# The last store of an attention decode kernel: one transfer of four rows against four transfers of one row from two engines

## The chip, the cores and the metric

The kernel runs on one core of a Trainium2 chip. The metric is the device time of one execution in microseconds (us). Times of whole executions come from repeated runs; everything finer comes from one profiled execution of each kernel. Two spans are used: the whole time, and **the tail**, which is the time from the end of VectorE's copy of the result to the end of the profiled span. The tail is all that the change can touch. An **issue** is the instruction by which an engine starts a transfer. A transfer's data leave in **packets**; in these stores each has a small packet beside it that writes a semaphore. A store is called **confirmed** here when that write has **landed**.

## The reference

One token passes through a layer normalisation; then the results of two branches are added to it: attention with 32 query heads over 8 cached key/value heads of 65,536 keys each, and a small feed-forward network.

```python
def reference(A_x, A_k_cache, A_v_cache, A_wq, A_wo, B_x, B_w1, B_b1, B_w2, B_b2):
    x = A_x                                  # (1, 1, 512) bf16
    xn = _layernorm(x, axis=-1)
    # _A_ref: q = xn @ wq; scores over 65536 cached keys; softmax; times V; @ wo
    # _B_ref: gelu(xn @ w1 + b1) @ w2 + b2
    return x + _A_ref(xn, A_k_cache, A_v_cache, A_wq, A_wo) + _B_ref(xn, B_w1, B_b1, B_w2, B_b2)
```

The caches hold 256 MiB; the output is 512 numbers of 2 bytes, 1 KB.

## The kernel before

The kernel streams keys and values through on-chip memory, and at the end multiplies the attention output with `wo`. The products go to four rows of one accumulator, at partitions 0, 32, 64 and 96, each row a quarter of the output. VectorE copies them to a tile `fin_bf`, and SyncE stores the four rows in one transfer:

```python
    for kt in range(KT):                                   # KT == 4
        ... pR[32 * kt:32 * kt + 1, 0:128] accumulates output columns kt*128 .. kt*128+127
    NR = 32 * (KT - 1) + 1
    sch.op(DVE, lambda: dve.tensor_copy(out=fin_bf[0:NR, :], in_=pR[0:NR, 0:128]),
           reads=[f"pss{R}"], writes=["fin"])
    ev_out = sch.dma(
        SP,
        lambda: sp.dma_start(out=out[0, 0].rearrange("(kt p) -> kt p", p=128), in_=fin_bf[0:NR:32, :]),
        sem_out, reads=["fin"], writes=["out_dram"],
    )
    # ... cut: the engines' programs are emitted in one block; what follows the
    # last placement of the attention output is emitted after it
    for e, obj in ((PE, pe), (DVE, dve), (SP, sp)):
        _emit(obj, e.ops[rest[e]:])
    sp.wait_ge(ev_out.sem, ev_out.val)
```

`sch.dma` and `sch.op` record an instruction with the semaphore waits that its reads and writes need. The kernel ends when SyncE's wait for the store's semaphore is over.

Of the kernel before, what the change touches and what calls it, by code (L numbers as in the profile page):

```python
# [154 lines left out]
def _fold(bodies, each):  # L155


    n = len(bodies)
    assert n >= 3 and all(len(b) == len(bodies[0]) for b in bodies)
    seen = {}  # L160
    for i, b in enumerate(bodies):
        for k, (waits, _, _) in enumerate(b):
            for s, v in waits:
                seen.setdefault((k, s), {})[i] = v
    growth = dict(each)
    for (_, s), at in seen.items():
        if n - 1 in at and n - 2 in at:
            assert growth.setdefault(s, at[n - 1] - at[n - 2]) == at[n - 1] - at[n - 2]
    out = []
    known = {}  # L170
    for k in range(len(bodies[0])):
        assert len({(b[k][2] or (None, 0))[1] for b in bodies}) == 1
        need = {}
        for (kk, s), at in seen.items():
            if kk == k:
                need[s] = max(v - i * growth.get(s, 0) for i, v in at.items())
        waits = [(s, v) for s, v in need.items() if known.get(s) is None or known[s] < v]
        for s, v in waits:
            known[s] = v
            assert v >= 1  # L180
        out.append((waits, bodies[0][k][1], bodies[0][k][2]))
    return out, growth


def _emit(eng_obj, ops):
    for waits, fn, pub in ops:
        for s, v in waits:
            eng_obj.wait_ge(s, v)
        if fn is None:
            continue  # L190
        ins = fn()
        if pub is not None:
            ins.then_inc(pub[0], pub[1])


def _emit_rolled(eng_obj, ops, marks, each, holder=None, step=None):
    folded, growth = _fold([ops[a:b] for a, b in zip(marks, marks[1:])], each)
    _emit(eng_obj, ops[:marks[0]])
    _emit_loop(eng_obj, folded, growth, len(marks) - 1, holder, step)
    _emit(eng_obj, ops[marks[-1]:])  # L200


def _emit_loop(eng_obj, ops, growth, n, holder, step):

    uses = {}
    for waits, _, _ in ops:
        for s, v in waits:
            uses.setdefault(s, []).append(v)
    regs, steps = {}, []
    at = {}  # L210
    for s, vs in uses.items():
        grow = growth.get(s, 0)
        key = (vs[0], grow) if len(vs) == 1 else s
        if key not in regs:
            r = eng_obj.alloc_register(f"w{len(regs)}")
            eng_obj.reg_mov(r, vs[0])
            regs[key] = r
            steps.append((r, vs[0] + grow - vs[-1]))
        at[s] = [regs[key], vs[0]]
    with eng_obj.Fori(0, n) as index:  # L220
        if holder is not None:
            holder[0] = index
        for waits, fn, pub in ops:
            for s, v in waits:
                r, now = at[s]
                if v != now:
                    eng_obj.reg_add(r, r, v - now)
                    at[s][1] = v
                eng_obj.wait_ge(s, r)
            ins = fn()  # L230
            if pub is not None:
                ins.then_inc(pub[0], pub[1])
        for r, by in steps:
            eng_obj.reg_add(r, r, by)
        if step is not None:
            step()
    if holder is not None:
        holder[0] = None


def bass_parallel_sum__gqa_block_cached__dense_activation_gelu__decode_kernel(
# [21 lines left out]
    KT = D // 128  # L263
# [23 lines left out]
    sch = _Sched(nc)  # L287
    PE = sch.add_engine("pe", "pe", is_pe=True)
    DVE = sch.add_engine("dve", "dve")
    ACT = sch.add_engine("act", "act")  # L290
    POOL = sch.add_engine("pool", "pool")
    SP = sch.add_engine("sp", "sp")
# [4 lines left out]
    pe = nc.tensor  # L297
    dve = nc.vector
    act = nc.scalar
    pool = nc.gpsimd  # L300
    sp = nc.sync

    def sb(name, shape, dt):
        return nc.alloc_sbuf_tensor(name, shape, dt)
# [34 lines left out]
    fin_bf = sb("fin_bf", [128, 128], BF)  # L339
# [57 lines left out]
    sem_w1 = sch.dsem("dw1")  # L397
    sem_w2 = sch.dsem("dw2")
    wsem = [sch.dsem(f"wsem{i}") for i in range(sum(len(s) for s in WS))]
    sem_out = sch.dsem("dout")  # L400

    for t, res in ((ident_bf, "ident_bf"), (ident_f, "ident_f")):
        sch.op(POOL, lambda t=t: pool.memset(t[:, :], 0.0), writes=[res])
# [3 lines left out]
                out=t[:, :], in_=t[:, :], compare_op=ALU.not_equal, fill=1.0,  # L407
                base=0, pattern=[[-1, 128]], channel_multiplier=1,
            ),
            reads=[res], writes=[res],  # L410
# [178 lines left out]
    def k_setup():  # L589
        trace = nc.cur_bb.bb.instructions  # L590
        n = len(trace)
        zero = pe.alloc_register("kzero")
        pe.reg_mov(zero, 0)
        tile = kv[:, bass.ds(pe.snap(zero, min_val=0, max_val=PCOL), DH)]
        kreg["ap"] = pe.transpose(pst[0][:, 0:128], tile, ident_bf[:, :]).ins.ins[1]
        assert trace[-2].outs[0].regref == kreg["ap"].regref
        kreg["at"] = trace[-2].ins[1].value
        del trace[n:]
        kreg["base"] = pe.alloc_register("kbase")
        kreg["both"] = pe.alloc_register("kboth")  # L600
        kreg["tile"] = [pe.alloc_register(f"ktile{r}") for r in range(NREG)]
        pe.reg_mov(kreg["base"], kreg["at"])
        pe.reg_mov(kreg["both"], 2 * kreg["at"] + 2 * PCOL)
# [159 lines left out]
    def place(w):  # L763
        ws = slice(w * WR, (w + 1) * WR)
        sch.op(PE, lambda: pe.matmul(pO[:, PO_X + w * WR:PO_X + (w + 1) * WR], lhsT=oM_bf[:, w, :],
                                     rhs=part_r[:, :], start=True, stop=True),
               reads=[f"oM{w}", "part_r"], writes=["pO0"])
        sch.op(DVX, lambda: dve.tensor_copy(out=oX_bf[:, ws], in_=pO[:, PO_X + w * WR:PO_X + (w + 1) * WR]),
               reads=["pO0"], writes=[f"oX{w}"])
# [52 lines left out]
    for t, res, pat in ((part_m, "part_m", "p (a r) -> p a r"), (part_r, "part_r", "p (a r) -> p r a")):  # L822
        sch.op(DVE, lambda t=t, pat=pat: dve.tensor_reduce(
            out=t[:, :], in_=ident_f[:, :].rearrange(pat, r=WR), axis=AX.X, op=ALU.max),
            reads=["ident_f"], writes=[res])
    marks, marks2 = [], []
    for i in range(NU // 2):
# [5 lines left out]
        each = {e.sem: e.count - was[e.sem] for e in (PE, DVE, ACT)}  # L833
# [10 lines left out]
    def fin_mm(kt, lhsT, rhs, reads, first, last, publish):  # L844
        sch.op(PE, lambda: pe.matmul(pR[32 * kt:32 * kt + 1, 0:128], lhsT=lhsT, rhs=rhs, start=first, stop=last),
               reads=reads, writes=[f"pss{R}"], publish=publish)
# [3 lines left out]
    for w in range(NW):  # L850
        if w:
            place(w)
            rest = {e: len(e.ops) for e in (PE, DVE, SP)}
        for r0, r1 in WS[w]:
            end = w == NW - 1 and r1 == WR
            for r in range(r0, r1):
                for kt in range(KT):
                    fin_mm(kt, oX_bf[:, w * WR + r:w * WR + r + 1], wo_sb[:, w * WR + r, kt * 128:(kt + 1) * 128],
                           [f"oX{w}", f"wo{w}_{r0}"], False, end and r == WR - 1, r == r1 - 1 and kt == KT - 1)
    NR = 32 * (KT - 1) + 1  # L860
    sch.op(DVE, lambda: dve.tensor_copy(out=fin_bf[0:NR, :], in_=pR[0:NR, 0:128]),
           reads=[f"pss{R}"], writes=["fin"])
    ev_out = sch.dma(
        SP,
        lambda: sp.dma_start(out=out[0, 0].rearrange("(kt p) -> kt p", p=128), in_=fin_bf[0:NR:32, :]),
        sem_out, reads=["fin"], writes=["out_dram"],
    )

    first, SP.ops[0] = SP.ops[0], ([], None, None)
    assert not first[0]  # L870
# [9 lines left out]
    with nc.Block() as block:  # L880

        @block.gpsimd
        def _(e):
            _emit(e, POOL.ops)

        @block.sync
        def _(e):
            _emit(e, SP.ops[:rest[SP]])

        @block.scalar  # L890
        def _(e):
            _emit_rolled(e, ACT.ops, [m[1] for m in marks2], each)

        @block.vector
        def _(e):
            _emit_rolled(e, DVE.ops[:rest[DVE]], [m[0] for m in marks2], each, pair)

        @block.tensor
        def _(e):
            k_setup()  # L900
            _emit_rolled(e, PE.ops[:rest[PE]], marks, each, step=k_step)

    for e, obj in ((PE, pe), (DVE, dve), (SP, sp)):
        _emit(obj, e.ops[rest[e]:])
    sp.wait_ge(ev_out.sem, ev_out.val)


# [26 lines left out]
```

## Time and profile before

| | before |
|---|---|
| time, median of 3 runs | 655.79 us (655.75 to 655.83) |
| profiled span | 654.3 us |
| read from memory | 280.50 MB at 429 GB/s |
| end of the result copy to the end of the span (tail) | 1.705 us |

The difference of some 1.5 us between time and span lies outside the profile's span. The page's DMA row and the chain, both shown in the prediction, say that the loads set the pace until about 651.6 us; after that there are eight matmuls, one copy and the store.

### The profile page before, as it was taken

Reading aid. Unit: us, or ns where it says so; the run is one execution under the profiler, and the core shown is the slowest. Engines: PE = TensorE matmul, PEld = TensorE weight load, DVE = VectorE, ACT = ScalarE, POOL = GpSimd, SP = SyncE. Lnnn points to the kernel's source line nnn. Section 1 sums busy time; section 2 is a strip of 40 time slices with the busy share of each in tenths; the row PEclk is TensorE's granted clock in tenths of the full one; section 3 lists DMA queues with packets and bytes.
Section 4 is the critical chain, followed back from the end, with each engine's and each line's share of the span. In section 5 each row is a group of like instructions: output and inputs, shape, how many; then the busy total and the mean of one; then the engine's idle time right before and its main releaser. Section 6 shows DMA issues by size and latency. Waiting matters only on the chain.

```text
span 654.3 us, 29016 instructions
## 1 busy us (share of the span) xinstructions
PE 530.7 (81%) x12681; PEld 504.3 (77%) x12681; DVE 280.6 (43%) x571; ACT 249.7 (38%) x454; POOL 5.6 (1%) x74
## 2 busy tenths in 40 slices
PE   2488498696969959697895969879596996998997
PEld 0187498696969959696895969779595986998996
DVE  3145063361625436162542616345261633645363
ACT  0134053351625425152451615335161543535351
POOL 0000000000000000000000000000000000000000
PEclk9688597695958869597885959779595887969695
DMA  9999999999999999999999999999999999999997
GB/s 386 445 430 439 415 452 431 421 441 441 429 441 421 441 429 441 425 437 449 421 425 441 441 425 433 433 441 433 437 425 437 433 441 421 425 445 421 427 439 310
DMA packets 6791, 280.66 MB, mean 429 GB/s; under 512 B 890, under 2 KB 1020, under 8 KB 1276
## 3 DMA queue, kind: packets, MB, share of 16 engines
q1 hardware_dynamic: 6632, 280.50, 99.4%
q8 instruction: 8, 0.13, 0.1%
q10 hardware_dynamic: 148, 0.01, 0.0%
q14 instruction: 3, 0.02, 0.0%
HBM read 280.50 MB, written 0.00 MB: 429 GB/s over the span
## 4 chain that ended last, share of the span: by engine, by line
DMA 57%; PE 33%; DVE 3%; another core or an unknown queue 3%; ACT 2%; issue 2%; SPq 1%; POOL 0%; ACTq 0%; DVEq 0%
DMA kv<-in_A_k_cache_dram 41%; PE pst L581 16%; DMA kv<-in_A_v_cache_dram 9%; DMA kv<-in_A_wo_dram 6%; PE pss L629 5%; PE pA L698 4%; PE pO L698 4%; DVE pmax L637 1%; DMA rows_bf<-in_A_x_dram 1%; PE pA L656 1%; ACT kt_ring L620 1%; PE pA L667 1%; DVE kt_ring L618 1%; PE pO L517 1%
## 5 line engine op out<-in xcount | busy, mean ns | idle before, releaser
L581 PE MATMUL pst<-ident_bf,kv 128*128 128x128 bf16 x4096 | 335.0, 233 | 87.2 <-POOL flag L449 84.6
L581 PEld LDWEIGHTS pst<-ident_bf,kv 128*128 x4096 | 261.7, 104 | 89.1 <-issue 89.0
L620 ACT ACTIVATE kt_ring<-pst 128x1024 bf16<-128x1024 bf16 x192 | 196.4, 1023 | 315.2 <-PE pst L581 300.3
L618 DVE COPY kt_ring<-pst 128x1024 bf16<-128x1024 bf16 x320 | 217.2, 690 | 222.5 <-PE pst L581 222.4
L629 PE MATMUL pss<-q_cur,kt_ring 128*128 128x4 bf16 x4096 | 174.5, 165 | 3.2 <-issue 1.7
L629 PEld LDWEIGHTS pss<-q_cur,kt_ring 128*128 128x128 bf16 x4096 | 153.9, 97 | 9.5 <-issue 5.5
L680 ACT ACTIVATE P_bf<-pss,negm 128x128 bf16<-128x128 f32 x128 | 57.1, 546 | 57.0 <-DVE negm L670 57.0
L698 PE MATMUL pO<-P_bf,kv 128*128 128x4 bf16 x2048 | 60.4, 166 | 5.8 <-issue 4.0
L698 PEld LDWEIGHTS pO<-P_bf,kv 128*128 128x128 bf16 x2048 | 56.5, 100 | 10.4 <-issue 8.3
L698 PEld LDWEIGHTS pA<-P_bf,kv 128*128 128x128 bf16 x2048 | 60.2, 106 | 4.7 <-issue 3.6
L698 PE MATMUL pA<-P_bf,kv 128*128 128x4 bf16 x2048 | 59.4, 167 | 4.5 <-issue 3.6
L680 ACT ACTIVATION_READ_ACCUMULATOR P_bf<-pss,negm 128x1 f32 x128 | 35.1, 274 | 0.0
L713 DVE COPY o_all<-pO 128x4 f32 (+1 forms) x16 | 2.6, 161 | 54.2 <-PE pO L720 54.2
L637 DVE TENSOR_REDUCE pmax<-pss 128x4 f32<-128x512 f32 x32 | 21.9, 685 | 7.2 <-PE pss L629 7.2
L713 DVE COPY o_all<-pA 128x4 f32 (+1 forms) x16 | 2.6, 161 | 38.2 <-PE pA L698 38.2
L656 PE MATMUL pA<-ident_f,pmax 128*4 128x128 f32 x64 | 13.0, 288 | 3.9 <-DVE pmax L637 2.6
L667 PE MATMUL pA<-diag,ones_f 4*128 4x4 f32 x64 | 13.6, 281 | 0.0
L658 DVE TENSOR_REDUCE gmax<-pA 4x1 f32<-4x128 f32 x32 | 8.8, 274 | 10.6 <-PE pA L656 10.6
L667 PEld LDWEIGHTS pA<-diag,ones_f 4*128 4x128 f32 x64 | 10.8, 210 | 2.0
L670 DVE TENSOR_SCALAR negm<-pA 128x4 f32<-128x4 f32 x32 | 5.2, 161 | 13.5 <-PE pA L667 13.5
L510 PE MATMUL pA<-ones_bf,xn_row 1*128 1x1 bf16 x4 | 0.3, 172 | 12.7 <-DVE xn_row L506 12.7
L510 PEld LDWEIGHTS pA<-ones_bf,xn_row 1*128 1x128 bf16 x4 | 0.2, 114 | 12.7 <-DVE xn_row L506 12.7
(78 smaller groups left out, 80.8 us busy)
## 6 DMA issues: line engine op xcount, KB each, us to landing
kv<-in_A_k_cache_dram SPq DMA_DIRECT2D x6, 4096.0 KB, 37.4
kv<-in_A_v_cache_dram SPq DMA_DIRECT2D x6, 4096.0 KB, 22.1
kv<-in_A_wq_dram SPq DMA_DIRECT2D x1, 4096.0 KB, 12.2
kv<-in_B_w_dram SPq DMA_DIRECT2D x2, 1792.0 KB, 17.7
kv<-in_A_wo_dram SPq DMA_DIRECT2D x1, 2048.0 KB, 34.5
kv<-in_A_wo_dram SPq DMA_DIRECT2D x1, 1152.0 KB, 36.8
kv<-in_A_wo_dram SPq DMA_DIRECT2D x1, 512.0 KB, 37.6
kv<-in_A_wo_dram SPq DMA_DIRECT2D x1, 256.0 KB, 37.8
```

What stands on the lines that cost most here:

```text
L517: sch.op(PE, lambda: pe.matmul(out, lhsT=lhsT, rhs=rhs, start=first, stop=last), reads=reads, writes=[res], publish=publish)
L581: ins = pe.transpose(pst[tb][:, at * 128:(at + 1) * 128], kslot[0][:, t, :], ident_bf[:, :]).ins
L618: e, fn = DVE, lambda tb=tb, dst=dst: dve.tensor_copy(out=dst, in_=pst[tb][:, :])
L620: e, fn = ACT, lambda tb=tb, dst=dst: act.activation(out=dst, in_=pst[tb][:, :], func=ACTF.Copy)
L629: lambda k=k, kb=kb, at=at, t=t: pe.matmul(pss[k][:, at:at + HPG], lhsT=kt_ring[:, kb * FCOL + t * 128:kb * FCOL + (t + 1) * 128], rhs=q_c ...
L637: lambda k=k: dve.tensor_reduce(out=pmax[:, :], in_=pss[k][:, 0:CW].rearrange("p (t j) -> p j t", j=HPG), axis=AX.X, op=ALU.max),
L656: sch.op(PE, lambda: pe.matmul(pA[0:HPG, PA_ST:PA_ST + 128], lhsT=pmax[:, 0:HPG], rhs=ident_f[:, :], start=True, stop=True), reads=["pmax" ...
L658: sch.op(DVE, lambda: dve.tensor_reduce(out=gmax4[:, :], in_=pA[0:HPG, PA_ST:PA_ST + 128], axis=AX.X, op=ALU.max), reads=["pA"], writes=[" ...
L667: sch.op(PE, lambda: pe.matmul(pA[:, PA_SB:PA_SB + HPG], lhsT=ones_f[0:HPG, 0:128], rhs=diag4[0:HPG, 0:HPG], start=True, stop=True), reads ...
L670: sch.op(DVE, lambda us=us: dve.tensor_scalar(out=negm[:, us], in0=pA[:, PA_SB:PA_SB + HPG], scalar1=-1.0, scalar2=None, op0=ALU.mult), re ...
L680: lambda: act.activation(out=P_v[k][:, :, j], in_=src[:, :, j], func=ACTF.Exp, bias=negm[:, at:at + 1], scale=1.0, accum_out=sums[:, at:at ...
L698: lambda k=k, t=t: pe.matmul(acc[:, 0:HPG], lhsT=vslot[:, k * TPD + t, :], rhs=P_v[k][:, t, :], start=t == 0, stop=t == TPD - 1),
```

## The change

The intent is to shorten the one issue of 0.64 us on SyncE: four transfers of a single row each, alternately issued by ScalarE and SyncE, so that each engine issues two. Each engine's transfers share a semaphore, and SyncE waits for both at the end.

```diff
-    sem_out = sch.dsem("dout")
+    sem_out = [sch.dsem(f"dout{i}") for i in range(2)]
...
-            rest = {e: len(e.ops) for e in (PE, DVE, SP)}
+            rest = {e: len(e.ops) for e in (PE, DVE, SP, ACT)}
...
-    ev_out = sch.dma(
-        SP,
-        lambda: sp.dma_start(out=out[0, 0].rearrange("(kt p) -> kt p", p=128), in_=fin_bf[0:NR:32, :]),
-        sem_out, reads=["fin"], writes=["out_dram"],
-    )
+    ev_out = []
+    for kt in range(KT):
+        e, q, sem = ((ACT, act, sem_out[1]), (SP, sp, sem_out[0]))[kt % 2]
+        ev = sch.dma(e, lambda kt=kt, q=q: q.dma_start(
+            out=out[0, 0:1, kt * 128:(kt + 1) * 128], in_=fin_bf[32 * kt:32 * kt + 1, :]),
+            sem, reads=["fin"], writes=[f"out{kt}"], total=KT // 2 * 16)
+        ev_out.append(ev)
...
-    for e, obj in ((PE, pe), (DVE, dve), (SP, sp)):
+    for e, obj in ((PE, pe), (DVE, dve), (ACT, act), (SP, sp)):
         _emit(obj, e.ops[rest[e]:])
-    sp.wait_ge(ev_out.sem, ev_out.val)
+    for ev in ev_out[:2]:
+        sp.wait_ge(ev.sem, ev.val)
```

(One further line keeps ScalarE's late instructions out of the block, as is done for the other engines.)

More of the change, by code (lines that the diff above doesn't have):

```diff
@@ L891, in _ @@
         def _(e):
-            _emit_rolled(e, ACT.ops, [m[1] for m in marks2], each)
+            _emit_rolled(e, ACT.ops[:rest[ACT]], [m[1] for m in marks2], each)
         @block.vector
```

## The prediction

> **What bounds the kernel now.** I read the page from the top, then the chain of work that ended last, then the timeline of the last microseconds, because the change touches only the very end.
>
> ```profile
> span 654.3 us, 29016 instructions
> ...
> DMA  9999999999999999999999999999999999999997
> ...
> HBM read 280.50 MB, written 0.00 MB: 429 GB/s over the span
> ## 4 chain that ended last, share of the span: by engine, by line
> DMA 57%; PE 33%; DVE 3%; another core or an unknown queue 3%; ACT 2%; issue 2%; SPq 1%; POOL 0%; ACTq 0%; DVEq 0%
> ```
>
> The DMA row is at nine tenths or more in 39 of 40 slices and 280.5 MB are read at 429 GB/s. The load stream sets the pace for some 650 us, and the change adds, moves or removes none of it. Only what follows the last load can change. The tail of the chain says when that is:
>
> ```profile
> 613.84 37.80 DMA kv<-in_A_wo_dram
> 651.64 0.04 issue
> 651.68 0.63 PE pss L845 x8
> 652.31 0.02 issue
> 652.33 0.29 DVE fin_bf L861
> ```
>
> (start us, us, what). The last piece of the output weight lands at about 651.64, eight matmuls run, and VectorE writes the result tile from 652.33 to 652.63. What comes after is the store, in the timeline of the end and in the list of what SyncE's queue waited for:
>
> ```profile
> 652.65 0.64 SPq L865 DMA_DIRECT2D out_dram<-fin_bf  x1
> ...
> SPq L865 <- DVE fin_bf L861: 3.1, 1, 3.1
> SPq L905 <- DMA out_dram<-fin_bf: 1.0, 1, 1.0
> ```
>
> SyncE starts the issue 0.03 us after VectorE ends, is busy with it for 0.64 us (637 ns by the listing of that tile), and then waits 1.0 us for the store's semaphore. So the store is 652.65 to 654.33, 1.68 us, all of it exposed: nothing else runs. That is 0.26% of 655.79 us. Even a store that took no time at all would not be faster by 2% (13.1 us), and a slower one would have to become nine times as long to be slower by 2%.
>
> **How the 1.68 us divide.** The transfer records of the trace show eight packets for this store: four of 256 bytes and four of 4 bytes (the semaphore writes). The first starts at 653.89, the last ends at 653.97. So:
> - issue on SyncE, 652.65 to 653.29: 0.64 us
> - end of the issue to the first packet: 0.60 us
> - the packets: 0.08 us (each data packet takes 15 to 16 ns)
> - last packet to the released wait, 653.97 to 654.33: 0.36 us
>
> The data are nothing; it is three latencies in a row.
>
> **What the Trainium skill says.**
> 1. "DMA: Bandwidth & Descriptors", section "Issuing engines are not separate DMA queues": transfers started by several engines run on the same 16 DMA engines, and starting them on several only saves sequencer time for the issue. So the change can at best act on the 0.64 us, and it does so by replacing one issue with two in a row on each of two engines.
> 2. Same page, "Why a DMA increments its semaphore by 16 and not by 1": the number of DMA engines follows from the slowest dimension that isn't 1, and a single row can go to only one. The trace agrees: the store of four rows has four pairs of packets, and ScalarE's queue has 148 packets for its three small loads, which is 128 of 28 bytes, 2 of 1024 and 18 semaphore writes (16 + 1 + 1). A one-row load is thus one packet and one semaphore write. Each new store should be one 256-byte packet and one 4-byte write: eight packets as before, two per semaphore and issuing engine pair, but all probably on one DMA engine in place of four. At 15 ns each that costs nothing visible; whether the receipts of the writes queue up on one engine no run here shows yet.
> 3. Same page, "Latency and other measured facts": about 600 ns to the first byte for transfers issued by SyncE or ScalarE. The trace has 0.60 us here, so it agrees; this part stays whatever the number of issues.
> 4. "Perfetto Trace Analysis", section "DMA Instruction — HWDGE (DVE, Sync)": the bar of an issue covers the wait for a descriptor generator that the two sequencers share, its use, and the excess semaphore increments. The two engines' issues may thus get in each other's way. In the trace this can be looked at only at the start of the kernel:
>
> ```profile
> 0.79 0.52 ACTq L457 DMA_DIRECT2D rows_bf<-in_A_x_dram  x1
> ...
> 0.80 0.33 SPq L470 DMA_DIRECT2D kv<-in_B_w_dram  x1
> 1.18 0.42 SPq L473 DMA_DIRECT2D kv<-in_B_w_dram  x1
> ...
> 1.34 0.21 ACTq L462 DMA_DIRECT2D rows_bf<-in_B_b_dram  x1
> ```
>
> Two issues that start within 0.01 us: SyncE's takes 0.33 us, ScalarE's one-row load 0.52, ending 0.18 after SyncE's. ScalarE's next one-row load took 0.21, though SyncE was issuing then too. So a one-row issue costs between 0.21 (unhindered) and 0.52 us (first, or hindered). These are the only durations for such a row in this trace, and they are loads, not stores.
>
> **The change part by part.**
> - The one issue of 0.64 us goes.
> - ScalarE gets two issues. It has been idle since 641.1 (its last activation starts at 640.82 and takes 0.32) and can start at the same 652.65 as SyncE, so they lie beside SyncE's. It passes the same end-of-block barrier as the others at about 649.5, three microseconds before it is needed; nothing moves there, for all its earlier instructions stay in the block.
> - SyncE gets two issues, 0.03 us apart (the gap between ScalarE's second and third issue at the start: 1.34 + 0.21 = 1.55, then 1.58). My central case takes the two measured one-row times in order: 0.52 + 0.03 + 0.21 = 0.76 us in place of 0.64, +0.12.
> - 0.60 to the first packet and 0.36 from the last packet stay; the first transfers' latencies lie beside the second issues.
> - SyncE ends with two waits in place of one. Such a wait takes 17 ns in the listing of the last line; with a gap of 0.03 us like the other gaps I put it at +0.04 us.
>
> Sum of the central case: 0.76 + 0.60 + 0.02 + 0.36 + 0.04 = 1.78 against 1.68, and rounded up for the small packets that land later, **+0.1 to +0.2 us**.
>
> **The rivals.**
> - **A: the long issue is due to the four-row shape.** The 128-row issues on SyncE after an idle wait take 0.33 us, a one-row issue 0.21; only the four-row one takes 0.64. If the shape is what costs, the new issues are 0.21 each, 0.21 + 0.03 + 0.21 = 0.45 against 0.64, and with the second wait the kernel ends 0.15 us sooner: 655.6. For it: 0.64 is out of line with every other issue. Against: this is also the only store and the only write to memory outside the core, so the shape is not the only difference.
> - **B: the long issue is due to its being a store (or the first use of the output), and the two engines hinder each other.** Then each engine's first issue stays at 0.64, and the second takes what back-to-back issues of SyncE take in this kernel, about 0.43: 0.64 + 0.03 + 0.43 = 1.10, +0.46, with the second wait +0.5. If the four also take turns fully, two more of 0.21 give +0.9. For it: ScalarE's 0.52 beside SyncE's 0.33. Against: the 0.21 that overlapped SyncE's 0.42 fully.
> - **C: four writes on one DMA engine wait for each other's receipts.** The time from packet to released wait is 0.36 us now; if the last write had to wait for one earlier receipt, up to +0.3 us on top. Against: they start staggered by the issues, so most of that is already past.
> - **D: nothing visible.** All of this is tenths of a microsecond; the three runs of before spread over 0.08 us, but another program may land elsewhere by more than that.
>
> **The range and the chances.** I give the central case (+0.15) about 40%, A (-0.15) 30%, B and C together (+0.5 to +0.9) 30%. The weighted mean is 0.06 - 0.045 + 0.2, about +0.2 us, so 656.0 us. The low end, 655.4, is A with 0.2 us of scatter between programs; the high end, 656.7, is full turn-taking of the four issues. Faster by over 2% is out of reach, as shown above; slower by over 2% would need a stall in ScalarE's late instructions of more than 13 us, or the slow load of another run.
>
> **What would show the steps right or wrong.** The load stream, the last matmuls and the result tile must end at the same time as now within a few tenths. The end of the trace must show two issues each on SyncE's and ScalarE's queue at line 866 or so, starting together right after VectorE's copy. Their durations decide: 0.52 then 0.21 for the central case, 0.21 twice for A, 0.64 and 0.43 for B. The packets must be four of 256 bytes, and the last wait about 0.36 us after the last of them; more than that speaks for C. The prediction would be wrong if ScalarE started its issues late, if one semaphore came far later than the other, or if the time before the result tile moved.

## The result

The changed kernel takes **655.76 us** (median of 6 runs, 655.61 to 655.88); the kernel before took 655.75 (6 runs, 655.64 to 655.83). The ratio is 1.0 with a 95% interval of 0.9987 to 1.0013. It is formed from the mean times, so it is not quite the ratio of these medians. The verdict is "same", which a change to a tail of 1.7 us could hardly have altered; what happened inside the tail has to be read from the traces.

The page of the changed kernel has the load stream as it was: 39 of 40 slices at nine tenths or more, the same bytes.

```profile
span 654.5 us, 29019 instructions
...
DMA  9999999999999999999999999999999999999997
...
HBM read 280.50 MB, written 0.00 MB: 429 GB/s over the span
```

The end of its timeline (start us, us, engine, line, operation) and what SyncE's queue waited for:

```profile
652.48 0.29 DVE L861 CAST fin_bf<-pss 97x128 bf16<-97x128 f32 x1 [3.03 <-PE pss L845]
652.80 0.63 SPq L866 DMA_DIRECT2D out_dram<-fin_bf  x2
652.81 0.55 ACTq L866 DMA_DIRECT2D out_dram<-fin_bf  x2
...
SPq L866 <- DVE fin_bf L861: 3.1, 1, 3.1
SPq L908 <- DMA out_dram<-fin_bf: 1.0, 1, 1.0
```

The two engines do start side by side, 0.005 us apart. But SyncE is busy with its two issues for 0.63 us, against 0.64 for the one before, and then waits 1.0 us as before. The listings of the result tile, first of the kernel before, then of the changed one, give each issue (ns, shortest/median/longest):

```profile
L865 SPq DMA_DIRECT2D out_dram<-fin_bf x1: 637/637/637, 652.7 to 652.7; - x1
```

```profile
L866 SPq DMA_DIRECT2D out_dram<-fin_bf x2: 255/288/322, 652.8 to 653.2; - x2
L866 ACTq DMA_DIRECT2D out_dram<-fin_bf x2: 249/262/276, 652.8 to 653.1; - x2
```

An issue of one row is about half as long as the issue of four, or less. The view of the DMA queues for 653.5 to 654.1 us of the changed kernel has the packets on two queues, four each (two data packets and two semaphore writes), each queue at 0.5% of the capacity of the sixteen DMA engines (q1 is SyncE's, q10 ScalarE's):

```profile
q1 hardware_dynamic: 4, 0.00, 0.5%
q10 hardware_dynamic: 4, 0.00, 0.5%
```

The tail is 1.698 us against 1.705. To see where the shorter issues went, one must go below the views, to the trace's records of packets and of semaphore writes that landed. All times here are us after the end of VectorE's copy; "lag" is from the start of a data packet to the landing of its semaphore write, in order of time on each queue. (The trace has one more landing per store, before its packets have left: at 1.038 before, and at 0.455, 0.470, 0.758 and 0.872 in the changed kernel. These are left out here and below.)

```
before   one issue, SyncE          changed    first    first    second   second
         row 1   2     3     4                ScalarE  SyncE    ScalarE  SyncE
issue    0.028 (all four)          issue      0.032    0.027    0.310    0.399
packet   1.260 1.273 1.287 1.319   packet     0.768    0.789    1.071    1.190
landed   1.608 1.620 1.633 1.671   landed     1.109    1.290    1.473    1.654
lag      0.348 0.347 0.346 0.352   lag        0.341    0.501    0.402    0.464
```

The last data packet leaves 0.13 us sooner than before. Only 0.01 of this comes from the issues, for SyncE's second one ends at 0.654 where the single one ended at 0.665. Some 0.06 comes from the time between the end of the issue and its first packet (0.536 against 0.595), and 0.06 from the fact that a one-row transfer has no further data packets behind the first (those of four rows were spread over 0.059). But in the changed kernel the landings are spaced 0.181, 0.183 and 0.181 us apart, whatever the spacing of the packets (0.021, 0.282, 0.119), and all but the first lag longer than 0.35. The last one lands only 0.017 us sooner than before, and the wait for two semaphores takes 0.028 us where the wait for one took 0.017. That leaves 0.006 us, which is the difference of the tails (0.007) but for rounding.

### The profile page after: what moved, and what is told of

Its sections match the earlier page's. It is cut to its first block, busy times and chain, and to the rows that moved or that the text cites. A ratio compares the mean times of both kernels' runs of the same rounds, so it can differ in the third digit from the quotient of the medians.

```text
span 654.5 us, 29019 instructions
## 1 busy us (share of the span) xinstructions
PE 530.4 (81%) x12681; PEld 504.3 (77%) x12681; DVE 280.8 (43%) x571; ACT 250.0 (38%) x454; POOL 5.7 (1%) x74
## 4 chain that ended last, share of the span: by engine, by line
DMA 57%; PE 33%; DVE 3%; another core or an unknown queue 3%; ACT 2%; issue 2%; SPq 0%; POOL 0%; ACTq 0%; DVEq 0%
DMA kv<-in_A_k_cache_dram 41%; PE pst L581 16%; DMA kv<-in_A_v_cache_dram 9%; DMA kv<-in_A_wo_dram 6%; PE pss L629 5%; PE pA L698 4%; PE pO L698 4%; DVE pmax L637 1%; DMA rows_bf<-in_A_x_dram 1%; ACT kt_ring L620 1%; PE pA L656 1%; PE pA L667 1%; DVE kt_ring L618 1%; PE pO L517 1%
```

## The experiments

My theory after this reading: the last row reaches the DMA sooner, but the four one-row stores have their writes confirmed one at a time, 0.18 us each, and the last store pays for the three ahead of it. The Trainium skill ("DMA: Bandwidth & Descriptors", section "Why a DMA increments its semaphore by 16 and not by 1") says that a transfer that uses k engines takes the lowest-numbered k, so four one-row stores would all be on the same engine, from whichever queue, if each uses one engine; each shows one data packet and one semaphore write. The trace doesn't name the engines of the packets. The rivals: one-row stores are simply confirmed later; the two issuing engines hinder each other; the number of writes counts wherever they are; the pattern is chance.

All runs gave a correct result except the four that are wrong, as said there; the runs with one execution have only their tails compared. Single executions scatter too much for tenths of a microsecond: the end of the result copy itself fell anywhere from 652.42 to 652.88 us in the kernels whose copy is unchanged.

### The changed kernel again

No edit.

> The changed kernel once more, unedited, to see whether the end repeats. From VectorE's result copy to the end of the span (the tail) the kernel before took 1.705 us, the changed one 1.698. My theory: the two-issue split does reach the DMA earlier (last packet 1.20 us after the copy against 1.33), but all four one-row stores use one DMA engine, and that engine confirms its writes one after another, 0.18 us apart (landings of the semaphore writes at 1.11, 1.29, 1.47 and 1.65 us), which gives the gain back. Expected: the spacing of 0.18 us again, tail 1.65 to 1.75. Rival (chance): landings not evenly spaced, the lag from packet to landing 0.35 us as before.

The tail was 1.693 us; the landings came at 1.103, 1.284, 1.467 and 1.648, again 0.181, 0.183 and 0.181 apart. The pattern is not chance. Whole time 655.99 us in one run, 656.07 for the kernel before beside it.

### All four stores from SyncE

```diff
-        e, q, sem = ((ACT, act, sem_out[1]), (SP, sp, sem_out[0]))[kt % 2]
+        e, q, sem = SP, sp, sem_out[0]
```

> All four one-row stores issued by SyncE. Theory of confirmations one after another (0.18 us apiece on one engine): SyncE's issues start some 0.3 us apart, wider than 0.18, so no store has to queue and each lag from data packet to landing falls back to about 0.35 us, as in the kernel before; the last issue ends 1.2 to 1.45 us after the copy, last packet 0.54 later, tail 2.1 to 2.4 us, that is 0.4 to 0.7 longer than with two engines. Rival (one-row writes are simply confirmed later, or the second wait costs): the lag stays at 0.40 to 0.50. Second question: if the issues of the two engines hinder each other in the changed kernel, SyncE's first issue alone is shorter than 0.32 us.

The tail was 2.100 us. The tile's listing:

```profile
L866 SPq DMA_DIRECT2D out_dram<-fin_bf x4: 238/254/323, 652.7 to 653.7; - x4
```

```
packet   0.777  1.126  1.420  1.719
landed   1.125  1.473  1.765  2.066
lag      0.348  0.347  0.345  0.347
```

Three things follow. With packets some 0.3 us apart the lag of every one-row store is back at 0.35, so such a store isn't confirmed later as such; it is the company that delays it. SyncE's first issue takes 0.323 us alone and 0.322 beside ScalarE's, and its second 0.256 and 0.255, so ScalarE doesn't lengthen SyncE's one-row issues (ScalarE's were not run alone). Yet after issues that end within 0.002 us of each other, SyncE's second packet left at 1.126 us here and at 1.190 and 1.184 in the two runs of the changed kernel. Beside ScalarE it is thus some 0.06 us late, after the bar; no run shows why. And the second issuing engine is worth 2.100 - 1.698 = 0.40 us: without it, the split would have made the end longer.

### The four-row store from ScalarE

The one transfer of the kernel before, moved to the other engine:

```diff
-    for kt in range(KT):
-        ... (four one-row stores)
+    ev = sch.dma(ACT, lambda: act.dma_start(
+        out=out[0, 0].rearrange("(kt p) -> kt p", p=128), in_=fin_bf[0:NR:32, :]),
+        sem_out[1], reads=["fin"], writes=["out_dram"])
```

> The one four-row store of the kernel before, issued by ScalarE in place of SyncE. If the 0.64 us belong to the four-row store, the issue is 0.60 to 0.66 us here too and the tail 1.65 to 1.75; if they belong to SyncE after its long wait, it is 0.25 to 0.35 and the tail 1.3 to 1.45. Landing lag 0.35 us, four landings within 0.07 us as in the kernel before[...].

```profile
L864 ACTq DMA_DIRECT2D out_dram<-fin_bf x1: 616/616/616, 652.6 to 652.6; - x1
```

The issue took 0.616 us and the tail 1.735. The long issue goes with the transfer and not with SyncE. (ScalarE had been idle for long too; but SyncE's first one-row issue, after the same wait as in the kernel before, took 0.322.) The four landings came within 0.066 us of one another, each 0.35 after its packet.

### Two stores of two rows

```diff
+    rows = out[0, 0].rearrange("(kt p) -> kt p", p=128)
+    for h in range(2):
+        e, q, sem = ((ACT, act, sem_out[1]), (SP, sp, sem_out[0]))[h]
+        ev = sch.dma(e, lambda h=h, q=q: q.dma_start(
+            out=rows[2 * h:2 * h + 2, :], in_=fin_bf[64 * h:64 * h + 33:32, :]),
+            sem, reads=["fin"], writes=[f"out{h}"])
```

> Two stores of two rows, one by ScalarE, one by SyncE. Theory: each store runs on two DMA engines, so an engine has two writes to confirm, not four, and only one can queue: lag 0.35 for the first pair and at most 0.35 + 0.18 for the second. An issue of two rows lies between the one-row 0.25 to 0.32 and the four-row 0.64. Tail 0.03 + 0.45 + 0.54 + 0.35 to 0.53 + 0.03 = 1.4 to 1.6 us, 0.1 to 0.3 shorter than either kernel. Rival (the confirmation time goes by number of writes on the chip, not on the engine): four landings 0.18 us apart again. Rival (the 0.64 us is a fixed cost of a store from several partitions): issue 0.6, tail 1.6 to 1.75.

This missed: the tail was 1.874 us, longer than both kernels. The issues were as long as the second rival had them, but its tail of 1.6 to 1.75 was passed too.

```profile
652.80 0.61 SPq L867 DMA_DIRECT2D out_dram<-fin_bf  x1
652.80 0.60 ACTq L867 DMA_DIRECT2D out_dram<-fin_bf  x1
```

Two rows cost nearly as much to issue as four (0.606 against 0.637 on SyncE, 0.604 against 0.616 on ScalarE), so the cost doesn't go by the number of rows. Besides, though the two bars lie side by side, ScalarE's packets left at 1.499 us, 0.27 after SyncE's at 1.229. "Perfetto Trace Analysis" (section "DMA Instruction — HWDGE (DVE, Sync)") describes a generator that is shared by the two sequencers and locked by the one that uses it. Its place for the wait for that lock is inside the bar of the issue; here the bars didn't grow and the packets came late all the same, so what held them is not settled by this run. The lag was 0.34 to 0.35 for all four. The two writes of one transfer landed about 0.01 us apart; the two transfers were 0.27 apart, more than 0.18, so this run doesn't test the pace.

### Four adjacent rows, and other steps

Three kernels with the one store of the kernel before, reading other rows of the tile. The output is wrong; size and shape of the transfer are the same.

```diff
-in_=fin_bf[0:NR:32, :]
+in_=fin_bf[0:KT, :]
```

> The kernel before with its one store reading rows 0 to 3 of the tile instead of rows 0, 32, 64, 96 (the result is wrong on purpose; shape and bytes are the same). If the step of 32 rows makes the issue long, it falls from 0.64 to 0.3 us and the tail after VectorE's copy from 1.705 to about 1.4 us. If several rows as such are what costs (two rows took 0.60 us, four 0.62 to 0.64, one 0.25 to 0.32), it stays at 0.60 to 0.65 and the tail at 1.65 to 1.75.

```profile
L865 SPq DMA_DIRECT2D out_dram<-fin_bf x1: 348/348/348, 652.8 to 652.8; - x1
```

The issue fell from 0.637 to 0.348 us, and the time from its end to the first packet from 0.595 to 0.430. The tail was 1.250 us, 0.455 shorter than before, which is the sum of the two (0.289 + 0.165) to within 0.001. The expectation had foreseen the first of them only, and so a tail of 1.4. So it is the step between the rows that makes the store long, twice over. Then steps of 2 and 8:

```diff
-in_=fin_bf[0:NR:32, :]
+in_=fin_bf[0:2 * KT - 1:2, :]            # step2
+in_=fin_bf[0:8 * (KT - 1) + 1:8, :]      # step8
```

> The kernel before with its one store reading rows 0, 2, 4, 6 of the tile (wrong on purpose). Rows 0 to 3 took 0.35 us to issue, rows 0, 32, 64, 96 took 0.64. If any step other than 1 makes the issue long, it is 0.60 to 0.65 and the tail 1.65 to 1.75 us; if the long issue comes from the distance (rows in different groups of 32), it is 0.35 and the tail 1.25.

> As the run with step 2, with rows 0, 8, 16, 24 (wrong on purpose): still within the first 32 rows. Any step: 0.60 to 0.65 us, tail 1.65 to 1.75. Only across groups of 32: 0.35 us, tail 1.25. A value in between would mean that the cost grows with the distance.

Each line is from the timeline of the end, the first of the step of 2, the second of the step of 8:

```profile
652.45 0.71 SPq L865 DMA_DIRECT2D out_dram<-fin_bf  x1
```

```profile
652.80 0.71 SPq L865 DMA_DIRECT2D out_dram<-fin_bf  x1
```

Both took 0.709 us, with tails of 1.789 and 1.796. That is more than I had expected for any step (0.60 to 0.65), and clearly not the short case. It isn't the distance that counts, nor a crossing of groups of 32 rows, but that the rows don't lie next to each other. Why these two steps cost 0.07 us more to issue than the step of 32 is not known.

### Sixteen adjacent rows

```diff
-rearrange("(kt p) -> kt p", p=128), in_=fin_bf[0:NR:32, :]
+rearrange("(a p) -> a p", p=32), in_=fin_bf[0:16, 0:32]
```

> The kernel before with its one store as sixteen rows of 64 bytes (rows 0 to 15 of the tile, wrong on purpose)[...]. If it is the use of fewer than 16 engines that makes the issue long, it falls to 0.33 us and the tail to about 1.4; if any store of several rows costs some 0.6 us, it is 0.60 to 0.70 and the tail 1.65 to 1.8. Landings within 0.1 us of one another in both cases, each 0.35 after its packet.

```profile
L865 SPq DMA_DIRECT2D out_dram<-fin_bf x1: 361/361/361, 652.6 to 652.6; - x1
```

The issue took 0.361 us and the tail was 1.421. By itself this could have been put down to the use of sixteen engines, as its expectation offered; but four adjacent rows took 0.348, so it is again the missing step. Its sixteen landings came about 0.012 us apart, from 1.212 to 1.387 (over 0.175 us, where 0.1 had been expected), all for rows of the same kilobyte. So neither the number of writes nor their common target sets a pace of 0.18 us.

### Sixteen one-row stores

```diff
+    for s in range(4 * KT):
+        kt, c = divmod(s, 4)
+        e, q, sem = ((ACT, act, sem_out[1]), (SP, sp, sem_out[0]))[s % 2]
+        ... out[..., kt*128 + c*32 : kt*128 + (c+1)*32] <- fin_bf[32*kt : 32*kt + 1, c*32 : (c+1)*32]
```

> The changed kernel with each row stored in four quarters: sixteen one-row stores of 64 bytes, eight per engine. Theory (one DMA engine confirms these writes one after another, 0.18 us apart): the first landing stays at 1.10 us after the copy, the others follow 0.18 apart, the last at 1.10 + 15 x 0.181 = 3.82, tail 3.8 to 3.9 us; the lag from packet to landing grows steadily to about 0.9. Rival (no queue, only issues count): SyncE's eighth issue starts at about 0.03 + 0.37 + 6 x 0.295 = 2.17, its packet comes 0.73 later and lands 0.35 after that, tail about 3.3 us, lag constant at 0.35 to 0.5.

The timeline (eight issues merged on each engine):

```profile
652.73 2.50 SPq L867 DMA_DIRECT2D out_dram<-fin_bf  x8
652.74 2.38 ACTq L867 DMA_DIRECT2D out_dram<-fin_bf  x8
```

The issues end 2.52 us after the copy, yet the tail is **3.864 us**. The sixteen stores landed from 1.087 to 3.819 us, (3.819 - 1.087) / 15 = 0.182 apart, the last 0.81 after its packet at 3.005. The last landing had been expected at 3.82; the rival's tail of 3.3 is excluded. In order, the landings of each queue were:

```
ScalarE  1.087  1.452  1.816  2.181  2.544  2.909  3.273  3.638
SyncE    1.269  1.633  1.997  2.361  2.726  3.090  3.455  3.819
```

Here the effect even shows in the whole time, though each is a single run: 657.99 us against 655.76 for the kernel before beside it, 2.23 us more where the tail grew by 2.16. The size of a write has no part in it: these had 64 bytes, those of the changed kernel 256, and the pace is the same.

What is shown is that single-row stores which reach the DMA from both queues in quick succession complete one at a time, 0.18 us each. That the reason is the one DMA engine they share is the skill's statement joined to this pattern. I found no way to put one-row stores on different engines, so this last link is argued, not shown. (Stores issued by GpSimd were not tried.) A rival is left beside it: wherever landings came 0.18 us apart, each followed one of the other queue, and in the one run with separate stores from a single queue they were never closer than 0.29 us. A pace set by the change from queue to queue would look the same, and no run here tells the two apart.

### The result gathered into two rows

From the two findings (avoid a step, have few one-row stores) follows a version with one short issue per engine: VectorE and ScalarE each copy two of the result rows into one row, in a part of the key buffer that is free by then.

```diff
-    sch.op(DVE, lambda: dve.tensor_copy(out=fin_bf[0:NR, :], in_=pR[0:NR, 0:128]),
-           reads=[f"pss{R}"], writes=["fin"])
+    fin2 = kt_ring[:, 0:256]
+    for kt in range(2):
+        ... DVE copy  fin2[0:1, kt*128:(kt+1)*128]   <- pR[32*kt : 32*kt + 1, 0:128]     writes "finA"
+    for kt in range(2):
+        ... ACT copy  fin2[64:65, kt*128:(kt+1)*128] <- pR[64 + 32*kt : 65 + 32*kt, 0:128]  writes "finB"
+    # SyncE stores fin2[0:1, :] to out[0:256], ScalarE stores fin2[64:65, :] to out[256:512]
```

> A version that follows from both findings: VectorE copies two result rows into one row, ScalarE the other two into another, and each is stored as one row of 512 bytes by SyncE and ScalarE: two short issues side by side and two writes to confirm. From the end of the last matmul (2.02 us before in the kernel before, 2.01 in the changed one): two copies in a row 0.02 + 2 x 0.29 + 0.03 = 0.63, then 0.03 to the issue, 0.74 from there to the packet, 0.35 + up to 0.18 to the landing, 0.03: 1.78 to 1.96 us, 0.05 to 0.25 shorter than both. If the one-row store of 512 bytes or ScalarE's copies cost more than thought, no gain. In the whole time no difference beyond the scatter between runs.

```profile
652.44 0.57 ACT L867 ACTIVATE kt_ring<-pss 1x128 bf16<-1x128 f32 x2 [10.89 <-PE pss L845]
652.44 0.60 DVE L863 CAST kt_ring<-pss 1x128 bf16<-1x128 f32 x2 [3.05 <-PE pss L845]
653.04 0.25 ACTq L873 DMA_DIRECT2D out_dram<-kt_ring  x1
653.07 0.32 SPq L873 DMA_DIRECT2D out_dram<-kt_ring  x1
```

Here the copies are part of what was changed, so the count starts at the start of the first copy: 652.44 to 654.34, 1.89 us (1.90 in the text below, which used the rounded times), against 2.00 in the kernel before (652.33 to 654.33) and 1.99 in the changed one (652.48 to 654.47). The end is 0.10 us shorter, as expected, and more than repeats of one kernel differ by (0.006 us for the changed kernel). The two stores landed 0.18 us apart once more (1.091 and 1.273 after VectorE's last copy). Then timed:

> The gathered version again, timed in five rounds. Its trace gave 1.90 us from the start of the first result copy to the end of the span, against 2.00 in the kernel before and 1.99 in the changed one. Expected: the same end in the trace within 0.03 us; in the whole time at most 0.1 us, which the scatter between runs hides, so same as before.

The trace repeated, with 652.43 to 654.32, 1.89 us. The time was 655.72 us (5 runs, 655.51 to 655.75), the kernel before 655.70 (9 runs, 655.55 to 655.89), ratio 0.9999 with an interval of 0.9985 to 1.0013. The gain is in the trace and is too small for the timing.

## Why the prediction was right or wrong

The measured 655.76 us lies in the range of 655.4 to 656.7. The range covers all the rivals. For the tail, the number of 656.0 us stood for +0.2 us and the central case for +0.1; measured was -0.007. Point by point:

**The bound.** Right. The store is the only part that differs, and the load stream ended as it had; the result copy came 0.15 us later, within the scatter of single executions (652.42 to 652.88).

**The issues.** The central case took 0.52 + 0.03 + 0.21 = 0.76 us from two loads at the start of the kernel. SyncE's two took 0.322 + 0.050 + 0.255 = 0.627, ScalarE's 0.249 + 0.029 + 0.276 = 0.554. This term was mis-sized by 0.13 us: I had read the 0.52 of a first load as the price of a first issue or of hindrance. SyncE's first issue was only 0.07 longer than its second, and no longer beside ScalarE than alone. None of the three pairs of durations named as signs (0.52 and 0.21, 0.21 twice, 0.64 and 0.43) came.

**The latencies.** The 0.60 us to the first packet "stay" didn't quite: it was 0.536 from the end of SyncE's last issue to its packet. The 0.36 at the end, which has the final wait of 0.017 in it, did not stay either: it became 0.459 + 0.028 = 0.487. The second wait cost 0.011 of this, not 0.04. With the measured terms the sum from the end of the copy is 0.027 + 0.627 + 0.536 + 0.021 + 0.459 + 0.028 = 1.698 us.

**Rival A** (the shape of four rows makes the issue long) named the right cause, though not closely enough: it is the step between rows, as the runs with adjacent rows and with steps of 2 and 8 show, not their number. Its sum of -0.15 us failed in two terms. It took 0.45 us for SyncE's two issues, from a one-row load of 0.21 on ScalarE, and they took 0.627: of the 0.19 it hoped for, 0.01 came. And it left the confirmations as they were, where the stretch from the last packet to the wait grew by 0.112 (0.347 to 0.459).

**Rival B** is refuted for one-row stores. The long issue isn't due to its being a store (adjacent rows: 0.348), and SyncE's first issue is as long alone as beside ScalarE's. What the two engines did to each other was outside the bars: some 0.06 us at SyncE's second packet.

**Rival C**, in effect if not in its reason (one engine), was the one that acted, and I had argued most of it away. The staggered issues were to keep the stores out of each other's way. They don't, because four stores reach the DMA within 1.190 - 0.768 = 0.42 us while three confirmations after the first take 0.54. It cost some 0.12 us at the last store (a lag of 0.464 against 0.347), where I had allowed up to 0.3.

So the division of the store into parts was right, but none of the cases had their sizes. Against the central case the issues were 0.13 us shorter and the time to the first packet 0.06 shorter, while the stretch from the last packet to the end of the wait was 0.09 longer (0.487 against 0.36 + 0.04). Together that is 0.11 less, from +0.10 to -0.007. None of the cases foresaw a tail all but unchanged, so it was luck that errors of opposite sign cancelled in part. The 656.0 us itself leaned on a share of 30% for B's +0.5 to +0.9, which nothing supported in the end.

## What to carry to other kernels

Before working on the last store, compare its tail with the whole: here 1.7 of 655 us, so that even its complete removal would have stayed below 2%. When one transfer is split into several, look at both ends of each: the bar of the issue gets shorter, but transfers of a single row that leave close together were confirmed one after another here, and that doesn't show in any bar. A store from rows that lie next to each other is worth more than the split: its tail was 1.25 us, against 1.70 for both kernels. But that run stored the wrong rows. The gathered version, which brings the right ones together, spent 0.30 us more on copies (0.60 against 0.29) and kept 0.10.

## What the Trainium skill lacked or had wrong

- "DMA: Bandwidth & Descriptors" doesn't give the cost of a step between the partitions that a transfer reads. One store of four rows took 0.348 us to issue from adjacent rows, 0.709 with steps of 2 and 8, and 0.637 with a step of 32; with a step of 32 the first packet also came 0.165 us later after the issue.
- The same page, in its section on the semaphore increment, says that an engine's semaphore write lands after its data, but not at what pace such writes follow each other. One-row stores from two queues landed about 0.18 us apart (four and sixteen stores, 256 and 64 bytes), where sixteen rows in one transfer landed 0.012 apart.
- The same page's section "Issuing engines are not separate DMA queues" says that a second engine saves only issue time, usually small beside the DMA itself. For 1 KB in four transfers the second engine took 0.40 us off a tail of 2.10.
- Its figure of about 0.6 us to the first byte agrees with the kernel before (0.595), counted from the end of the issue; the page doesn't say from where it counts. Counted so, it is high for one-row stores (0.43 to 0.54) and adjacent rows (0.430).
- "Perfetto Trace Analysis" puts the wait for the shared generator inside the bar of the issue. With two two-row stores at once, bars of 0.606 and 0.604 us lay side by side while the packets of one left 0.27 us after those of the other.
